# Fused attention, Fourier mixing, MLP and gated convolution: who multiplies and who adds the five taps of the gate's causal convolution

## The chip, the cores and the metric

The kernel runs on one core of a Trainium2 chip. The metric is the device time of one execution in microseconds (us), lower is better. TensorE (PE in the profile) does the matrix products, VectorE (DVE), ScalarE (ACT) and GpSimd (POOL) the element-wise work, and SyncE (SP) issues the DMA transfers.

## The reference

Three layers, one behind the other, on 4 batch entries of 576 positions and 512 features.

```python
x = out_up + out_local        # attention over pooled q, k, v, plus a band of 7 keys around each position
u = x + real(fft(fft(x, axis=1), axis=2))
un = (u - mu) / sqrt(var + 1e-06)
x = u + maximum(un @ w_ch1, 0) @ w_ch2              # 512 -> 2048 -> 512
xp = concatenate([zeros(B, 4, D), x], axis=1)
gate_pre = sum over k in 0..4 of conv_w[k] * xp[:, k:k + S, :]
gate = 1 / (1 + exp(-gate_pre))
out = (gate * (x @ w_val)) @ w_out
```

The convolution is depthwise and causal: tap k multiplies the signal shifted by 4 - k positions with one weight for each feature, so tap 4 is the position itself.

## The kernel before

**Layout.** Features lie on the 128 partitions, in 4 blocks of 128; X holds the 576 positions of a batch entry behind 4 columns of zeros. All the work behind the attention goes in 12 *units*, (b, j) for 4 batch entries and 3 pieces of UT = 192 positions. W is a list of 128x1024 weight tiles; the matrices are split into two fp16 halves each, and a product takes three passes of matmuls. W_n in the lists of instructions is such a tile; a weight piece that goes from the raw 64-bit form to float32 (`to_f32`) takes three VectorE instructions, one of line 283 (a shift and a mask) and two `stt` (line 165 is the `stt` helper, `scalar_tensor_tensor`; line 171 is the `add` helper, line 168 `mul`). `conv_w` then scales a piece and splits it.

**A unit's MLP** (`mlp_steps`). `h_group(g)`, g = 0 to 7, makes 24 matmuls of ph; ScalarE writes the upper half hh of its relu, VectorE the lower half hl with one `stt` that reads PSUM and hh. `c_group(g)`, 24 matmuls of pc with hh and hl, stands two h_groups behind, so TensorE runs c_group(0), h_group(2), c_group(1) and so on. Unit 0 is of another form (`steps32`, lines 1009 and 1022): float32 products without hh and hl. So the first hl is unit 1's.

**A unit's gated convolution** (`moe2_steps`). `conv(t)` is called for t = 4, 0, 1, 2, 3. Tap 4 starts the sum g; each call makes four products of 128x192, one for each block of features. In the units 1 to 10 the sum lies in the last weight tile, W_121 in the rows; in the first and the last unit it lies in a buffer of the pool `tap`. That pool has 3 buffers, which the products of the taps, the fp16 pair yy (`split_y`, line 1099 and an `stt`) and the output tile osb share. Then come `sigm`, `val(0)` and `val(1)` (24 matmuls each with yy; an `stt` that multiplies with the gate; the pair gh, gl), and `out_tile` (products with w_out, osb, and the store to out_dram). The last unit alone, by `LASTV`, already multiplies and adds on VectorE.

**What lies between.** The convolution of a unit lies in the MLP of the next one, unit 0's taps thus at the beginning of unit 1. The attention, Fourier and normalization steps of the batch entries 1 to 3 are put between the units. In the low-resolution attention, sc are scores in PSUM, nm their negated maximum, E the exponentials by ScalarE (line 682), then eT and po. `pooled_v` sums pieces of v in three additions on GpSimd (vr, ptv; line 171) and squares each loaded piece (v, v4 and a number) on ScalarE (line 425) behind that. In the Fourier part fs are sums and differences, fF folds (line 787), FH and FL their fp16 pair, which TensorE takes as ab. The normalization (`ln`) has uc, sq, sums st and two Newton steps r on VectorE; its column sums lie on GpSimd in most units. In the units 0 and 1 the rest of the weights comes in too: w_val and w_out by tiles raw, in two buffers, converted by VectorE.

**What sets the order.** Each step has a position in `put` and `spread`; the steps are called by position, and the scheduler of the framework then orders the instructions of each engine by a timeline of its own, with the operands' and buffers' dependencies as semaphores. Each engine runs its own list in order. All loads and stores are issued by SP, in order too: an issue that waits for a buffer holds up those behind it.

Of the kernel before, what the change touches and what calls it, by code (L numbers as in the profile page):

```python
# [9 lines left out]
F32 = mybir.dt.float32  # L10
# [3 lines left out]
AF = mybir.ActivationFunctionType  # L14
ALU = mybir.AluOpType
AX = mybir.AxisListType

B, H, S, D = 4, 8, 576, 64
# [3 lines left out]
UT = 192  # L22
UPB = S // UT
# [50 lines left out]
LASTV = True  # L74
# [53 lines left out]
def attn_moe_kernel(ctx, tc, q_t, k_t, v_t, w1, w2, w_val, conv_t, w_out, c_feat, c_seq, c_band, c_eye, out):  # L128
    nc = tc.nc
    P = 128  # L130
# [21 lines left out]
    V, A, G, T = nc.vector, nc.scalar, nc.gpsimd, nc.tensor  # L152
# [11 lines left out]
    def stt(eng, out, in0, scalar, in1, op0, op1):  # L164
        return eng.scalar_tensor_tensor(out=out, in0=in0, scalar=scalar, in1=in1, op0=op0, op1=op1)  # L165
# [4 lines left out]
    def add(eng, out, a, b):  # L170
        return eng.tensor_tensor(out=out, in0=a, in1=b, op=ALU.add)  # L171
# [24 lines left out]
    cw = const.tile([P, 4, 5], F32, name="cw")  # L196
# [717 lines left out]
    mainp = {}  # L914
# [173 lines left out]
    def moe2_steps(b, j):  # L1088
        i = b * UPB + j
        steps = []  # L1090
        m_ = {}
# [11 lines left out]
        def conv(t):  # L1103
            X = st[b]["X"]
            st[b]["taps"] = st[b].get("taps", 0) + 1
            c0 = PAD + j * UT - 4 + t
            if t == 4:
                if i in (0, B * UPB - 1):
                    g = mainp["tap"].tile([P, 4, UT], F32, tag="tap", name="tap")
                else:  # L1110
                    g = W[NPOS][:, 0:4 * UT].rearrange("p (a t) -> p a t", a=4)
            elif not (LASTV and i == B * UPB - 1):
                g = mainp["tap"].tile([P, 4, UT], F32, tag="tap", name="tap")
            last = LASTV and i == B * UPB - 1
            for c in range(4):
                if last and t == 4:
                    V.tensor_scalar(out=g[:, c], in0=X[:, c, c0:c0 + UT], scalar1=cw[:, c, t:t + 1], scalar2=None,
                                    op0=ALU.mult)
                elif last:
                    m = m_["g"][:, c]  # L1120
                    stt(V, m, X[:, c, c0:c0 + UT], cw[:, c, t:t + 1], m, ALU.mult, ALU.add)
                else:
                    A.activation(out=g[:, c], in_=X[:, c, c0:c0 + UT], func=AF.Copy, scale=cw[:, c, t:t + 1])  # L1123
            if last and t < 4:
                return
            if t == 4:
                m_["g"] = g
            else:
                add(G, m_["g"], m_["g"], g)

        def sigm():
            A.activation(out=m_["g"], in_=m_["g"], func=AF.Tanh, scale=0.5)
# [49 lines left out]
        def sof(b):  # L1182
# [4 lines left out]
            return d["sof"]  # L1187

        taps = [scale_out] + [lambda t=t: conv(t) for t in (4, 0, 1, 2, 3)] + [sigm]
        vals = [lambda: val(0), lambda: val(1)]  # L1190
        if i < B * UPB - 2:
# [59 lines left out]
    c0, c1 = st[0]["cuts"]  # L1251
# [101 lines left out]
```

## Time and profile before

| | before |
|---|---|
| median of 3 runs (lowest to highest) | 771.54 us (769.82 to 771.86) |
| the profiled execution, its own time | 768.35 us |
| its span | 766.5 us |
| mean granted TensorE clock | 0.93 |
| busy: PE / DVE / ACT / POOL | 91% / 59% / 49% / 24% |

The span goes from the first to the last instruction that the profiler saw in one execution; busy shares are shares of it. The granted clock is 1.00 at the upper level of TensorE's clock, 2.4 GHz, and 0.50 at the lower one, 1.2 GHz. Up to about 185 us the first attention, the loading of weights and unit 0 run. The first hl of the units 1 to 11 start at 197, 250, 306, 366, 429, 482, 538, 592, 632, 673 and 712 us.

### The profile page before, as it was taken

What the parts mean: (1) busy time and instruction counts of PE and PEld (TensorE: products, weight loads), DVE (VectorE), ACT (ScalarE), POOL (GpSimd) and SP (SyncE); (2) the same over time, 40 slices, a digit from 0 to 9 for tenths busy, and PEclk for the clock granted to TensorE, in tenths of its full rate; (3) what the DMA queues carried; (4) which work ended last, traced back from release to release, by engine and by line L of the source; (5) the groups of instructions that cost most, each with busy time, mean ns of one, the idle gap of its engine ahead of it and who ended that gap; (6) DMA issues with size and microseconds to landing.
All of it is one profiled execution on the core that took longest, in us unless ns stands there. A gap on an engine that the chain in (4) does not pass through costs nothing.

```text
span 766.5 us, 18498 instructions
## 1 busy us (share of the span) xinstructions
PE 695.8 (91%) x7811; PEld 605.4 (79%) x7811; DVE 450.3 (59%) x897; ACT 378.1 (49%) x1170; POOL 183.8 (24%) x187
## 2 busy tenths in 40 slices
PE   6869579986699998999979999898999999999996
PEld 3535459985688987987869899788799998999893
DVE  3894789769885766256786631656742472532134
ACT  1465211778544636677552766864522435251512
POOL 0400000015421522361231243601410323030300
PEclk8565579999799999999999999999899999999999
DMA  9965347033321110222121001001100000000001
GB/s 227 370 226 166 112 185 208 24 101 117 102 74 56 55 64 16 54 93 77 39 69 64 16 23 34 22 2 54 55 15 2 16 1 30 2 15 2 29 1 42
DMA packets 29004, 54.79 MB, mean 71 GB/s; under 512 B 2133, under 2 KB 17109, under 8 KB 27898
## 3 DMA queue, kind: packets, MB, share of 16 engines
q1 hardware_dynamic: 28922, 53.61, 21.6%
q8 instruction: 61, 1.00, 0.5%
q14 instruction: 21, 0.17, 0.1%
HBM read 46.52 MB, written 9.45 MB: 73 GB/s over the span
## 4 chain that ended last, share of the span: by engine, by line
PE 61%; DVE 20%; ACT 8%; DMA 7%; issue 1%; SPq 1%; POOL 0%; ACTq 0%; DVEq 0%; POOLq 0%
PE pc L1065 19%; PE ph L1047 18%; DVE W L165 6%; PE val L1144 5%; PE out L1160 5%; ACT dP L536 3%; PE po L716 2%; DMA v<-in_v_dram 2%; DVE W L283 2%; DVE fF L787 1%; ACT tap L1123 1%; PE dO L577 1%; PE sc L668 1%; DMA raw<-in_moe_w_out_dram 1%; PE ab L810 1%
## 5 line engine op out<-in xcount | busy, mean ns | idle before, releaser
L1065 PE MATMUL pc<-hh,W 128*128 128x192 f16 x1408 | 199.4, 248 | 3.8 <-ACT hh L1051 3.8
L1065 PEld LDWEIGHTS <-W 128*128 128x128 f16 x2112 | 178.0, 99 | 25.6 <-issue 21.8
L1047 PE MATMUL ph<-uh,W 128*128 128x192 f16 x1408 | 196.4, 247 | 0.1
L1065 PE MATMUL pc<-hl,W 128*128 128x192 f16 x704 | 173.3, 249 | 12.7 <-DVE hl L165 12.7
L1047 PEld LDWEIGHTS <-W 128*128 128x128 f16 x2112 | 176.4, 98 | 7.1 <-issue 5.1
L1047 PE MATMUL ph<-ul,W 128*128 128x192 f16 x704 | 173.7, 247 | 0.0
L171 POOL TENSOR_TENSOR W<-W,tap 128x768 f32<-128x768 f32 x40 | 74.9, 1873 | 141.2 <-ACT tap L1123 109.8
L165 DVE SCALAR_TENSOR_TENSOR hl<-ph,hh 128x384 f16<-128x384 f32 x88 | 48.0, 551 | 98.4 <-ACT hh L1051 98.2
L1051 ACT ACTIVATE hh<-ph 128x384 f16<-128x384 f32 x88 | 42.3, 485 | 72.0 <-PE ph L1047 71.6
L1123 ACT ACTIVATE tap<-X,cw 128x192 f32<-128x192 f32 x180 | 66.5, 446 | 5.5 <-DMA out_dram<-osb 4.7
L1144 PE MATMUL val<-yy,W 128*128 128x192 f16 x576 | 53.3, 246 | 4.0 <-ACT yy L1099 2.3
L1144 PEld LDWEIGHTS <-W 128*128 128x128 f16 x576 | 48.0, 98 | 5.1 <-issue 3.9
L536 ACT ACTIVATE dP<-dS,dmx 128x64 f32<-128x64 f32 x160 | 47.7, 332 | 0.3
L1160 PE MATMUL out<-W,gh 128*128 128x512 f16 x144 | 45.9, 379 | 0.0
L536 ACT ACTIVATION_READ_ACCUMULATOR dP<-dS,dmx 128x1 f32 x160 | 36.2, 226 | 0.0
L1160 PE MATMUL out<-W,gl 128*128 128x512 f16 x72 | 27.3, 379 | 2.1 <-DVE gl L165 2.1
L165 DVE SCALAR_TENSOR_TENSOR W<-W,W 128x1024 int32<-128x1024 int32 x24 | 28.7, 1215 | 0.1
L171 POOL TENSOR_TENSOR vr<-v 72x256 f32<-72x256 f32 x12 | 11.3, 944 | 66.9 <-DMA v<-in_v_dram 64.2
L165 DVE SCALAR_TENSOR_TENSOR yy<-X,s_y,yy 128x768 f16<-128x768 f32 x12 | 19.2, 1601 | 13.5 <-ACT yy L1099 13.4
L682 ACT ACTIVATE E<-sc,nm 72x144 f32<-72x144 f32 x64 | 23.5, 372 | 4.8 <-PE po L716 4.7
L716 PE MATMUL po<-ET,vr 72*64 72x144 f32 x128 | 21.6, 345 | 4.6 <-ACT ET L711 4.6
L1009 PE MATMUL ph<-u,W 128*128 128x192 f32 x128 | 24.8, 350 | 1.0 <-DVE u L945 1.0
(222 smaller groups left out, 1212.4 us busy)
## 6 DMA issues: line engine op xcount, KB each, us to landing
W<-in_moe_w_ch_dram SPq DMA_DIRECT2D x12, 1024.0 KB
v<-in_v_dram SPq DMA_DIRECT2D x32, 144.0 KB
out_dram<-osb SPq DMA_DIRECT2D x18, 256.0 KB
vw<-in_v_dram SPq DMA_DIRECT2D x16, 256.0 KB
X<-in_q_dram SPq DMA_DIRECT2D x6, 576.0 KB
kT<-in_k_dram SPq DMA_DIRECT2D x4, 582.0 KB
dx<-X SPq DMA_DIRECT2D x4, 576.0 KB
dr<-dx SPq DMA_DIRECT2D x4, 576.0 KB
```

The source lines that it names most:

```text
L165: return eng.scalar_tensor_tensor(out=out, in0=in0, scalar=scalar, in1=in1, op0=op0, op1=op1)
L171: return eng.tensor_tensor(out=out, in0=a, in1=b, op=ALU.add)
L536: A.activation(out=s_[:, z, a], in_=pss[par][:, z, a], func=AF.Exp, scale=SCALE, bias=mx[:, par, z, a:a + 1], accum_out=su[:, par, z, a:a ...
L682: A.activation(out=E[:, qc], in_=ps[:, qc], func=AF.Exp, scale=SCALE / 16, bias=nm[:, qc:qc + 1], accum_out=su[:, qc:qc + 1],)
L716: T.matmul(out=po[par * 64:par * 64 + 64], lhsT=d["vr"][:, kc, (a % 2) * 4 + (a // 2) * 2 + par], rhs=ets[par][:, kc], start=(kc == 0), st ...
L1009: i = T.matmul(out=ps[:, e], lhsT=W[kc * 2 + m // 8 + 1][:, o:o + 128], rhs=u()[:, kc, :], start=(kc == 0), stop=(kc == 3))
L1047: T.matmul(out=ps[:, e], lhsT=w1_ap(pw, kc, 2 * g + e), rhs=uh[px][:, kc, :], start=(t == 0), stop=(t == 11))
L1051: A.activation(out=h_, in_=ps, func=AF.Relu)
L1065: T.matmul(out=ps[m // 2][:, m % 2], lhsT=w2_ap(pw, kk, m), rhs=x[px][:, e, :], start=(kk == 0 and (pw, px) == (0, 0) and m % 2 == 0), sto ...
L1123: A.activation(out=g[:, c], in_=X[:, c, c0:c0 + UT], func=AF.Copy, scale=cw[:, c, t:t + 1])
L1144: T.matmul(out=ps[:, e], lhsT=wv_ap(pw, kc, 2 * mh + e), rhs=m_["y"][px][:, kc, :], start=(t == 0), stop=(t == 11))
L1160: T.matmul(out=ps, lhsT=(gh, gl)[px][:, kc, t * 128:(t + 1) * 128], rhs=wo_ap(pw, kc), start=(n == 0), stop=(n == 11))
```

## The change

The taps 0 to 3 are no longer multiplied by ScalarE into a buffer of their own and added by GpSimd: VectorE does both with one `stt` for each block of features, in place, out = x * w + out. Tap 4 stays ScalarE's product (VectorE's in the last unit, as before). The buffers for the four other products fall away.

```diff
--- before.py
+++ after.py
@@ -1109,24 +1109,16 @@
                     g = mainp["tap"].tile([P, 4, UT], F32, tag="tap", name="tap")
                 else:
                     g = W[NPOS][:, 0:4 * UT].rearrange("p (a t) -> p a t", a=4)
-            elif not (LASTV and i == B * UPB - 1):
-                g = mainp["tap"].tile([P, 4, UT], F32, tag="tap", name="tap")
+                m_["g"] = g
             last = LASTV and i == B * UPB - 1
             for c in range(4):
-                if last and t == 4:
-                    V.tensor_scalar(out=g[:, c], in0=X[:, c, c0:c0 + UT], scalar1=cw[:, c, t:t + 1], scalar2=None,
-                                    op0=ALU.mult)
+                x, w, m = X[:, c, c0:c0 + UT], cw[:, c, t:t + 1], m_["g"][:, c]
+                if t < 4:
+                    stt(V, m, x, w, m, ALU.mult, ALU.add)
                 elif last:
-                    m = m_["g"][:, c]
-                    stt(V, m, X[:, c, c0:c0 + UT], cw[:, c, t:t + 1], m, ALU.mult, ALU.add)
+                    V.tensor_scalar(out=m, in0=x, scalar1=w, scalar2=None, op0=ALU.mult)
                 else:
-                    A.activation(out=g[:, c], in_=X[:, c, c0:c0 + UT], func=AF.Copy, scale=cw[:, c, t:t + 1])
-            if last and t < 4:
-                return
-            if t == 4:
-                m_["g"] = g
-            else:
-                add(G, m_["g"], m_["g"], g)
+                    A.activation(out=m, in_=x, func=AF.Copy, scale=w)
 
         def sigm():
             A.activation(out=m_["g"], in_=m_["g"], func=AF.Tanh, scale=0.5)
```

The scheduler orders the lists anew. Three places are shown; lines behind the edit have numbers lower by 8 in the changed kernel.

VectorE around the first hl, that of unit 1, before (tap is the gate's sum or a product, W_117 and W_118 are pieces of w_ch2, W_120 and W_121 pieces of w_val and w_out on their way from raw):

```order
L165 SCALAR_TENSOR_TENSOR W_117<-W_118,s_w_1528,W_117 128x1024
L165 SCALAR_TENSOR_TENSOR W_120<-raw,W_120 128x512 x2
L283 TENSOR_SCALAR W_120<-raw 128x512
L165 SCALAR_TENSOR_TENSOR W_120<-raw,W_120 128x512 x2
L945 TENSOR_TENSOR uc<-X,st 128x768
L283 TENSOR_SCALAR W_121<-raw 128x512
L165 SCALAR_TENSOR_TENSOR W_118<-W_118,s_w_1528 128x1024
L165 SCALAR_TENSOR_TENSOR hl<-ph,hh 128x384
```

and of the change:

```order
L165 SCALAR_TENSOR_TENSOR W_117<-W_118,s_w_1528,W_117 128x1024
L165 SCALAR_TENSOR_TENSOR tap<-X,cw,tap 128x192 x3
L165 SCALAR_TENSOR_TENSOR W_120<-raw,W_120 128x512
L165 SCALAR_TENSOR_TENSOR tap<-X,cw,tap 128x192 x4
L165 SCALAR_TENSOR_TENSOR W_120<-raw,W_120 128x512
L165 SCALAR_TENSOR_TENSOR tap<-X,cw,tap 128x192 x2
L945 TENSOR_TENSOR uc<-X,st 128x768
L165 SCALAR_TENSOR_TENSOR W_118<-W_118,s_w_1528 128x1024
L165 SCALAR_TENSOR_TENSOR tap<-X,cw,tap 128x192
L283 TENSOR_SCALAR W_120<-raw 128x512
L165 SCALAR_TENSOR_TENSOR hl<-ph,hh 128x384
```

Ten multiply-adds now stand ahead of this hl; the shift of W_121 moved behind it, and the second shift of W_120 stands right in front of it.

TensorE at the same place, as a difference (pc_2100 is the accumulator whose second matmul reads hl):

```order
 L1047 LDWEIGHTS W_114
 L1047 MATMUL ph<-uh,W_114 128x192
-L939 MATMUL st<-uc,ones 128x192
 L1065 LDWEIGHTS W_115
 L1065 MATMUL pc_2100<-hh,W_115 128x192
 L1065 LDWEIGHTS W_115
 L1065 MATMUL pc_2101<-hh,W_115 128x192
+L668 MATMUL sc<-qkT 72x144 x4
 L1065 LDWEIGHTS W_115
 L1065 MATMUL pc_2100<-hl,W_115 128x192
```

A sum of squares' or means' st moved forward, and four score products sc stand ahead of the first matmul that reads hl. ScalarE at the same place, as a difference (v_1851 is a loaded piece of v, ssv its sum of squares):

```order
 L1051 ACTIVATE hh<-ph 128x384
-L1123 ACTIVATE tap<-X,cw 128x192 x4
-L1051 ACTIVATE hh<-ph 128x384
-L1123 ACTIVATE tap<-X,cw 128x192 x4
-L951 ACTIVATE sq<-uc 128x768
-L682 ACTIVATE E,lsu<-sc,nm 72x144
 L425 ACTIVATE v_1851,ssv<-v_1851 72x512
-L682 ACTIVATE E,lsu<-sc,nm 72x144
+L682 ACTIVATE E,lsu<-sc,nm 72x144 x4
 L425 ACTIVATE v_1862,ssv<-v_1862 72x512
```

Eight products of taps are gone from here, and the four exponentials E stand in one piece behind the square of v_1851.

SP's list of loads at the same time, before (v4 are pieces of v, raw those of the raw weights):

```order
L186 DMA v4_1808<-in_v_dram 72x2x256
L188 DMA v4_1850<-in_v_dram 72x2x256
L188 DMA raw_2095<-in_moe2_w_val_dram 128x1024
L188 DMA raw_2259<-in_moe2_w_out_dram 128x1024
L188 DMA v4_1851<-in_v_dram 72x2x256
L188 DMA v4_1862<-in_v_dram 72x2x256
L188 DMA raw_2230<-in_moe2_w_val_dram 128x1024
```

and of the change:

```order
L186 DMA v4_1808<-in_v_dram 72x2x256
L188 DMA v4_1850<-in_v_dram 72x2x256
L188 DMA v4_1851<-in_v_dram 72x2x256
L188 DMA raw_2095<-in_moe2_w_val_dram 128x1024
L188 DMA v4_1862<-in_v_dram 72x2x256
L188 DMA v4_1863<-in_v_dram 72x2x256
L188 DMA raw_2259<-in_moe2_w_out_dram 128x1024
L188 DMA raw_2230<-in_moe2_w_val_dram 128x1024
```

v4_1851 moved in front of raw_2095, and v4_1862 and v4_1863 in front of raw_2259.

VectorE in one of the late units, from the end of the unit ahead (X takes the sums pc), before:

```order
L165 SCALAR_TENSOR_TENSOR X<-pc_8650,iv_1544,X 128x2x192
L165 SCALAR_TENSOR_TENSOR X<-pc_8651,iv_1544,X 128x2x192
L165 SCALAR_TENSOR_TENSOR hl<-ph,hh 128x384 x3
L165 SCALAR_TENSOR_TENSOR yy<-X,s_y_9134,yy 128x768
L165 SCALAR_TENSOR_TENSOR hl<-ph,hh 128x384 x2
L165 SCALAR_TENSOR_TENSOR W_121<-W_121,val 128x384
```

and of the change:

```order
L165 SCALAR_TENSOR_TENSOR X<-pc_8584,iv_1544,X 128x2x192
L165 SCALAR_TENSOR_TENSOR X<-pc_8585,iv_1544,X 128x2x192
L165 SCALAR_TENSOR_TENSOR W_121<-X,cw,W_121 128x192 x7
L165 SCALAR_TENSOR_TENSOR hl<-ph,hh 128x384
L165 SCALAR_TENSOR_TENSOR W_121<-X,cw,W_121 128x192 x4
L165 SCALAR_TENSOR_TENSOR hl<-ph,hh 128x384
L165 SCALAR_TENSOR_TENSOR W_121<-X,cw,W_121 128x192 x5
L165 SCALAR_TENSOR_TENSOR yy<-X,s_y_9062,yy 128x768
L165 SCALAR_TENSOR_TENSOR hl<-ph,hh 128x384 x3
```

The sixteen multiply-adds stand among the first hl of the unit, in pieces of seven, four and five.

## Rows read from the trace of the kernel before

**Rows 1.** The page, busy time and share of each engine.

```profile
PE 695.8 (91%) x7811; PEld 605.4 (79%) x7811; DVE 450.3 (59%) x897; ACT 378.1 (49%) x1170; POOL 183.8 (24%) x187
```

**Rows 2.** Windows of 40 us; the first row names the columns.

```profile
core 0: us, PE busy (x) PEld busy (x) DVE busy (x) ACT busy (x) POOL busy (x), PEclk, DMA share, GB/s
160.00:200.00 40.00, 25.20 (x284) 23.05 (x283) 32.77 (x37) 33.27 (x97) 17.28 (x13) 0.81 0.27 90
...
360.00:400.00 40.00, 34.70 (x385) 30.47 (x384) 31.02 (x49) 22.16 (x60) 12.77 (x8) 1.00 0.18 52
...
520.00:560.00 40.00, 36.15 (x376) 31.76 (x374) 26.87 (x43) 19.61 (x45) 13.23 (x12) 0.91 0.18 59
...
600.00:640.00 40.00, 40.00 (x444) 37.27 (x443) 24.19 (x41) 17.15 (x37) 12.39 (x11) 1.00 0.02 9
```

**Rows 3.** Timeline, TensorE: start, length, instruction [idle before, its releaser].

```profile
197.55 0.32 PE L1065 MATMUL pc<-hl,W 128*128 128x192 f16 x1 [9.33 <-DVE hl L165]
```

**Rows 4.** Timeline, VectorE, 177 to 198 us.

```profile
177.18 1.28 DVE L165 SCALAR_TENSOR_TENSOR W<-W,s_w 128x1024 f16<-128x1024 f32 x1
...
180.97 0.41 DVE L283 TENSOR_SCALAR W<-raw 128x512 int32<-128x512 int32 x1
...
182.50 1.82 DVE L165 SCALAR_TENSOR_TENSOR W<-raw,W 128x512 int32<-128x512 int32 x2
184.77 2.86 DVE L283 TENSOR_SCALAR W<-raw 128x512 int32<-128x512 int32 x1 [0.45 <-DMA raw<-in_moe_w_val_dram]
...
190.90 0.94 DVE L945 TENSOR_TENSOR uc<-X,st 128x768 f32<-128x768 f32 x1
191.76 2.53 DVE L283 TENSOR_SCALAR W<-raw 128x512 int32<-128x512 int32 x1
194.21 2.82 DVE L165 SCALAR_TENSOR_TENSOR W<-W,s_w 128x1024 f16<-128x1024 f32 x1
196.95 0.55 DVE L165 SCALAR_TENSOR_TENSOR hl<-ph,hh 128x384 f16<-128x384 f32 x1
```

**Rows 5.** Timeline, GpSimd, 181 to 196 us.

```profile
181.78 1.99 POOL L171 TENSOR_TENSOR vr<-v 72x256 f32<-72x256 f32 x1 [8.22 <-DMA v<-in_v_dram]
...
185.55 3.75 POOL L171 TENSOR_TENSOR tap<-tap 128x768 f32<-128x768 f32 x2
...
192.20 3.75 POOL L171 TENSOR_TENSOR tap<-tap 128x768 f32<-128x768 f32 x2
```

**Rows 6.** Groups by line: instruction and count | busy, mean ns | idle before.

```profile
L1123 ACT ACTIVATE tap<-X,cw 128x192 f32<-128x192 f32 x180 | 66.5, 446 | 5.5 <-DMA out_dram<-osb 4.7 <-POOL W L171 0.5 <-DVE X L165 0.2
...
L1123 ACT ACTIVATE W<-X,cw 128x192 f32<-128x192 f32 x40 | 15.8, 449 | 19.0 <-DVE X L165 17.8 <-DVE gl L165 0.9 <-DVE W L165 0.4
...
L171 POOL TENSOR_TENSOR W<-W,tap 128x768 f32<-128x768 f32 x40 | 74.9, 1873 | 141.2 <-ACT tap L1123 109.8 <-ACT W L1123 30.3
...
L165 DVE SCALAR_TENSOR_TENSOR tap<-X,cw,tap 128x192 f32<-128x192 f32 x16 | 5.7, 405 | 0.0
```

**Rows 7.** Chain of waits, 180 us: start, length, what.

```profile
180.05 4.70 DMA raw<-in_moe_w_val_dram
```

**Rows 8.** Timeline, SP's issues of v.

```profile
178.26 0.33 SPq L186 DMA_DIRECT2D v<-in_v_dram  x1
...
184.89 1.89 SPq L188 DMA_DIRECT2D v<-in_v_dram  x2
```

**Rows 9.** Timeline, ScalarE, an exponential.

```profile
192.62 0.36 ACT L682 ACTIVATE E<-sc,nm 72x144 f32<-72x144 f32 x1
```

**Rows 10.** Window behind the wait for hl, columns as in rows 2.

```profile
197.50:202.20 4.70, 4.65 (x30) 4.39 (x30) 4.18 (x10) 2.69 (x7) 0.32 (x1) 0.50 0.32 106
```

**Rows 11.** Timeline, VectorE, two Newton steps.

```profile
388.32 0.35 DVE L165 SCALAR_TENSOR_TENSOR r<-r,r 128x192 f32<-128x192 f32 x1
...
389.10 1.87 DVE L165 SCALAR_TENSOR_TENSOR r<-r,vv 128x192 f32<-128x192 f32 x1
```

**Rows 12.** Timeline, ScalarE, products of a tap at 395 us.

```profile
395.21 1.49 ACT L1123 ACTIVATE tap<-X,cw 128x192 f32<-128x192 f32 x4 [3.92 <-DMA out_dram<-osb]
```

**Rows 13.** Chain of waits, late unit, one group of matmuls.

```profile
678.94 1.98 PE pc L1065 x24
```

## The prediction, made before the changed kernel ran

> **What bounds the kernel now.** I read the page's busy shares first, then stretches of 40 us, then what TensorE waited for, then VectorE, GpSimd and ScalarE around each such wait. TensorE is busy 91% of the span and VectorE, the next, 59% [rows 1]. Those are averages over stages. In the late units TensorE has no gap at all: 40.00 us of 40 between 600 and 640, while VectorE is busy 24.2, ScalarE 17.2 and GpSimd 12.4 [rows 2]. There a change on the other engines can only cost, never gain. Between 160 and 200 TensorE works 25.20 us of 40, between 360 and 400 it works 34.70, between 520 and 560 it works 36.15 [rows 2]. That is 14.8, 5.3 and 3.85 us of idle time, and whatever this change brings has to come out of such stretches. In the third, VectorE is held up by GpSimd's differences and squares, which stay; I count nothing for it, nor for the smaller gaps between.
>
> The large gap is one wait: at 197.55 a matmul of pc starts that had waited 9.33 us for hl from VectorE [rows 3], that is since 188.22. VectorE was never idle before that hl. It was slow. A shift (line 283) that takes 0.41 us at 180.97 takes 2.86 at 184.77 and 2.53 at 191.76; a weight conversion that takes 1.28 at 177.18 takes 2.82 at 194.21 [rows 4]. GpSimd is at work in all these moments: a sum of v, then two tap additions from 185.55 to 189.3, two more from 192.20 to 195.95 [rows 5]. So the four tap additions of unit 0 hold VectorE up, and TensorE with it. The Trainium skill ("SBUF — State Buffer", Who interferes with whom) gives this a rule: a VectorE instruction in a two-port mode or with two SBUF inputs and a GpSimd instruction that reads SBUF exclude each other for a whole instruction. The 2.86 against 0.41 agrees with it.
>
> **The change, part by part.** *ScalarE* loses 16 of 20 products in each of 11 units. 220 took 66.5 + 15.8 = 82.3 us, so 0.374 each [rows 6], and 176 of them are 65.8 us. ScalarE was not what TensorE waited for in the large gap, so I count nothing for this by itself.
>
> *GpSimd* loses all 44 additions: 74.9 us for forty [rows 6] and two pieces of 3.75 for the other four [rows 5], 82.4 us in all. GpSimd's own time is on no path that I found; what counts is that VectorE is no longer held by them.
>
> *VectorE* gains 176 multiply-adds. The last unit already does this work there: 16 of them in 5.7 us, 0.356 each [rows 6]. That is 62.7 us, 5.7 per unit. In the full stretches it lies beside TensorE's work (VectorE 24.2 + 5.7 of 40 [rows 2]); without that cover it would be 5.7 us a unit.
>
> *Unit 0's taps, the gap at 188.* They lie in unit 1's beginning. The order after shows ten of the sixteen multiply-adds ahead of the first hl, and one shift and one weight piece now behind it. Three things can be last.
> First, VectorE's queue. From 182.50 it has two weight pieces (1.82, the measured time, in part already held), ten multiply-adds (3.56), uc (0.94), a conversion (1.28) and a shift (0.41): 8.0 us, so hl starts at 190.5 instead of 196.95 [rows 4]. TensorE started 0.60 us after hl did, so it resumes at 191.1.
> Second, on SP the load of raw_2095, which that shift reads, now stands behind v4_1851. It was issued at 180.05 and took 4.70 [rows 7]. v4_1851 could not be issued before 184.89, when its buffer came free [rows 8]; so raw_2095 lands at 189.6 or a little later, and hl starts at 190.0. This is just covered.
> Third, TensorE now has the next four score matmuls (sc) ahead of the first matmul with hl, and their PSUM buffers are freed by ScalarE's exponentials, which stand behind the square of v4_1851. A v load issued at 178.26 was used at 181.78, 3.5 us later [rows 5, 8]; so v4_1851 is there at 188.4, its sum on GpSimd takes up to 1.99 [rows 5], four exponentials at 0.36 [rows 9] make 191.8, and 193.9 if the load and the sum are as slow again as they were quick here.
> TensorE thus resumes between 191.1 and 193.9. I take 192.75, near the later end, since the third chain has the most links: a gain of 4.8 us (3.6 to 6.4).
>
> *The clock behind that gap.* From 197.5 to 202.2 TensorE's granted clock is 0.50, the lower of its two levels (1.2 of 2.4 GHz) [rows 10]: 4.7 us of work that would have been 2.35 at the upper one. It fell during the idle 9.33 us. The idle time will be about half as long; whether the clock then falls no row tells. Bounds 0 and 2.35, taken 1.2.
>
> *Units 3 and 4, 360 to 400.* Here a Newton step of the normalization that takes 0.35 at 388.32 takes 1.87 at 389.10, and the one after it the like [rows 11], under two tap additions on GpSimd; they stand in front of the FL that TensorE waits for. And ScalarE stands 3.92 us until an output store frees a tap buffer, then makes four products (1.49) before yy, which TensorE waits for next [rows 12]. Both causes are gone: the additions, and the buffers that each tap took from the pool that output and yy also use. The first is worth two times 1.5 us. Bounds: 0, if GpSimd's half of the transform is as late, and 5.3, the whole idle time of the stretch [rows 2]. Taken 3.0.
>
> *What the multiply-adds cost elsewhere.* In the late units seven stand in a row ahead of an hl: 2.5 us. A block of hl is wanted two groups of 24 matmuls after its turn, and a group takes 1.98 [rows 13], so there are about 4.0 us. Seven alone are covered. They read two SBUF tiles, and where GpSimd works at the same moment they can be held as the Newton step was, 1.5 us each time: 2.5 + 1.5 = 4.0 is just covered, two such holds lose 1.5. I take one such loss, 1.5 us in all, in the range from 0 to one per unit.
>
> **Sum.** The profiled execution took 768.35 us, 1.85 around its span of 766.5. 768.35 - 4.8 - 1.2 - 3.0 + 1.5 = 760.85. The runs shown have their median at 771.54, 3.19 above it, so I forecast 764.0. Taking all lower bounds (6.4 + 2.35 + 5.3, no loss) gives 757.5 on that scale.
>
> **Rivals.**
> *The wait only moves (no change).* Line 283's shift of the next raw weights stands in VectorE's queue ahead of later hl, and on SP raw_2259 goes from two places ahead of v4_1862 to behind v4_1863. If that load lands late, TensorE, ahead by 5 us at 193, waits for a later hl instead and has lost the lead by about 225. Then 4.8 + 1.2 go and 1.5 net of the rest stays: 770.0. For it: each raw load takes 4.70 us and there are only two buffers [rows 7]. Against it: the order also moves other work of VectorE in front, and TensorE has no wait that long anywhere behind 200 in which the loads show. The Trainium skill's "Perfetto Trace Analysis" (Optimizing Scalar/DVE Operations) warns in the same direction: the two engines share an SBUF port, so handing work from one to the other might not help. By that sentence, too, about nothing would change.
>
> *VectorE is held in every unit (slower).* One mechanism: the multiply-adds ahead of hl, held by what GpSimd still does (sums of v, squares, the transform's differences, normalizations). If each of the ten units behind the first has two holds, it loses 1.5 us, 15 us in all against 9.0 gained: 774.35, or 777.5 on the scale of the median. It decides from 0.9 us per unit on. By the rule of the page "SBUF — State Buffer" in the Trainium skill every multiply-add is exposed to such a hold, since it has two SBUF inputs. For it: the 1.87 against 0.35 [rows 11] is such an instruction. Against it: GpSimd is left with little in the late units, where TensorE is full and VectorE idle for 40% [rows 2].
>
> *More than forecast.* All gaps close and the clock stays up: 757 or below.
>
> **Chances.** A median within 0.3%, 2.3 us, can't be told from no change. Forecast (757.5 to 769.2): 0.66. More than that: 0.04. The wait only moves, or gains and holds cancel (769.2 to 773.9): 0.15. Held in every unit, or a like loss (above 773.9): 0.15. Faster 0.70, same 0.15, slower 0.15. The likeliest case has its range from 757 to 769; the range that leaves out no more than 2 in 10 goes from 757 to 774.
>
> **What would show it.** In the profile after: multiply-adds at about 0.36 each on VectorE and no tap additions on GpSimd; the line 283 shift back at 0.4 us around 185 to 192 except beside sums of v; the wait for hl of 9.33 us down to 3 to 6; less than 2.5 us of lower clock behind it; between 360 and 400 TensorE busy for 37 us or more; 600 to 640 still full. I would be wrong if a new wait of several us for hl or a raw load shows between 195 and 230, if the sc matmuls hold TensorE past 194, or if short waits for hl show in each late unit with multiply-adds of more than 1 us in front of them.

## The result, and the profile after

The changed kernel took 750.85 us (median of 4, 750.29 to 754.8) against 770.68 for the kernel before: a ratio of 0.9757, 95% interval 0.9716 to 0.9797. Run once more beside the later experiments it took 752.54 (ratio 0.9786, 0.9771 to 0.9801). The gain is thus 16.5 to 20 us. The prediction was 764.0, with a range of 757 to 774: right in sign, wrong in size by 13 us and outside its range.

The page of the changed kernel, busy times, answers to [rows 1]. ScalarE has lost 57 us and GpSimd 76, VectorE gained 32:

```profile
PE 688.4 (92%) x7811; PEld 599.7 (80%) x7811; DVE 482.2 (64%) x1073; ACT 321.0 (43%) x994; POOL 108.2 (14%) x143
```

The multiply-adds alone were to add 63 us to VectorE. Its count grew by just these 176 (897 to 1073), its busy time by half of that, so its other instructions took less time than before. Windows of 40 us of the changed kernel (columns as in [rows 2]; the stretches hold somewhat earlier work than those of before, since the kernel runs ahead):

```profile
160.00:200.00 40.00, 31.16 (x357) 28.23 (x356) 33.33 (x60) 29.57 (x83) 15.06 (x13) 0.91 0.23 75
360.00:400.00 40.00, 39.77 (x448) 35.48 (x446) 31.74 (x59) 15.29 (x31) 7.66 (x12) 1.00 0.25 82
440.00:480.00 40.00, 34.94 (x452) 31.42 (x450) 20.25 (x44) 21.06 (x66) 13.53 (x17) 0.91 0.07 22
520.00:560.00 40.00, 39.80 (x435) 35.02 (x433) 27.57 (x60) 13.41 (x28) 6.29 (x13) 1.00 0.11 35
600.00:640.00 40.00, 40.00 (x444) 37.04 (x443) 21.65 (x46) 12.53 (x22) 4.26 (x6) 1.00 0.04 15
```

TensorE's idle time between 360 and 400 is gone (5.30 to 0.23), that between 520 and 560 as well (3.85 to 0.20), and the late unit is as full as it was. One stretch, 440 to 480, has become worse (0.83 us of idle time before, 5.06 now). What TensorE waited for from 175 to 748 us, summed by releaser, before (us in total, times, longest):

```profile
PE pc L1065 <- DVE hl L165: 12.7, 4, 9.3
PE pc L1065 <- ACT hh L1051: 3.8, 2, 2.0
PE ab L810 <- DVE FL L165: 3.6, 2, 2.6
PE st L939 <- ACT X L583: 2.4, 3, 1.6
PE val L1144 <- ACT yy L1099: 2.3, 2, 1.3
```

and in the changed kernel:

```profile
PE pc L1065 <- DVE hl L165: 5.1, 2, 3.5
PE st L939 <- ACT X L583: 4.6, 3, 4.0
...
PE ph L1047 <- ACT uh L973: 1.6, 1, 1.6
...
PE pc L1065 <- ACT hh L1051: 1.2, 1, 1.2
...
PE ab L810 <- DVE FL L165: 0.2, 1, 0.2
```

The waits for hl fell by 7.6 us, those for FL by 3.4, those for yy are gone, those for hh fell by 2.6. A wait for ScalarE's X grew. VectorE ahead of the first hl, in the changed kernel (start, length; answers to [rows 4]):

```profile
179.06 0.41 DVE L283 TENSOR_SCALAR W<-raw 128x512 int32<-128x512 int32 x1
...
180.58 1.54 DVE L165 SCALAR_TENSOR_TENSOR tap<-X,cw,tap 128x192 f32<-128x192 f32 x3
182.05 1.21 DVE L165 SCALAR_TENSOR_TENSOR W<-raw,W 128x512 int32<-128x512 int32 x1
183.18 1.86 DVE L165 SCALAR_TENSOR_TENSOR tap<-X,cw,tap 128x192 f32<-128x192 f32 x4
...
189.56 0.95 DVE L283 TENSOR_SCALAR W<-raw 128x512 int32<-128x512 int32 x1
190.43 0.55 DVE L165 SCALAR_TENSOR_TENSOR hl<-ph,hh 128x384 f16<-128x384 f32 x1
```

The shifts of line 283 take 0.41 and 0.95 us; those of 2.5 to 2.9 are gone. TensorE waits twice here, first for X, then briefly for hl:

```profile
183.24 0.69 PE L939 MATMUL st<-uc,ones 128*128 128x192 f32 x1 [4.00 <-ACT X L583]
...
191.03 0.24 PE L1065 MATMUL pc<-hl,W 128*128 128x192 f16 x1 [1.60 <-DVE hl L165]
```

### The profile page after: what moved, and what is told of

It is laid out like the page before. It is cut to its first block, busy times and chain, and to the rows that moved or that the text cites. A ratio compares the mean times of both kernels' runs of the same rounds, so it can differ in the third digit from the quotient of the medians.

```text
span 749.1 us, 18445 instructions
## 1 busy us (share of the span) xinstructions
PE 688.4 (92%) x7811; PEld 599.7 (80%) x7811; DVE 482.2 (64%) x1073; ACT 321.0 (43%) x994; POOL 108.2 (14%) x143
## 4 chain that ended last, share of the span: by engine, by line
PE 59%; DVE 22%; DMA 9%; ACT 6%; POOL 2%; issue 1%; SPq 1%; DVEq 0%; POOLq 0%; ACTq 0%
PE pc L1065 20%; PE ph L1047 19%; DVE W L165 8%; PE out L1152 5%; PE val L1136 5%; ACT dP L536 3%; DMA v<-in_v_dram 2%; PE po L716 2%; DVE tap L165 2%; PE ab L810 1%; DMA dr<-dx 1%; DMA dx<-X 1%; DMA X<-in_moe_w_ch_dram 1%; DMA raw<-in_moe_w_ch_dram 1%; DVE fF L787 1%
## 5 line engine op out<-in xcount | busy, mean ns | idle before, releaser
L1065 PE MATMUL pc<-hh,W 128*128 128x192 f16 x1408 | 196.1, 247 | 1.2 <-ACT hh L1051 1.2
L1065 PEld LDWEIGHTS <-W 128*128 128x128 f16 x2112 | 176.7, 98 | 14.4 <-issue 10.8
L165 DVE SCALAR_TENSOR_TENSOR W<-X,cw,W 128x192 f32<-128x192 f32 x160 | 61.0, 437 | 2.3 <-ACT W L1121 2.2
L1152 PEld LDWEIGHTS <-gh 128*128 128x128 f16 x144 | 14.2, 99 | 14.4 <-issue 0.9
L1009 PE MATMUL ph<-u,W 128*128 128x192 f32 x128 | 24.3, 345 | 1.0 <-DVE u L945 1.0
L668 PE MATMUL sc<-qkT 64*72 64x144 f32 x128 | 22.4, 341 | 2.5 <-DVE qkT L588 1.0
L1143 ACT ACTIVATE gh<-W 128x384 f16<-128x384 f32 x20 | 10.6, 528 | 31.9 <-DVE W L165 31.8
L1121 ACT ACTIVATE W<-X,cw 128x192 f32<-128x192 f32 x40 | 15.5, 455 | 19.6 <-DVE X L165 17.8
```

The costliest lines, as they stand in the source:

```text
L668: T.matmul(out=pss[par][:, qc], lhsT=d["qkT"][r, 0, a, qc * QC:(qc + 1) * QC], rhs=d["qkT"][r, 1, a, :], start=True, stop=True,)
L1009: i = T.matmul(out=ps[:, e], lhsT=W[kc * 2 + m // 8 + 1][:, o:o + 128], rhs=u()[:, kc, :], start=(kc == 0), stop=(kc == 3))
L1065: T.matmul(out=ps[m // 2][:, m % 2], lhsT=w2_ap(pw, kk, m), rhs=x[px][:, e, :], start=(kk == 0 and (pw, px) == (0, 0) and m % 2 == 0), sto ...
L1121: A.activation(out=m, in_=x, func=AF.Copy, scale=w)
L1152: T.matmul(out=ps, lhsT=(gh, gl)[px][:, kc, t * 128:(t + 1) * 128], rhs=wo_ap(pw, kc), start=(n == 0), stop=(n == 11))
```

## The experiments

A ratio below is always to the kernel before, on the same chip and in the same hour. Of each edit only the lines that matter are shown; the pool of the buffer `dum` is left out.

**Which engine's relief is it?** First the two halves of the change, each alone. *add_on_dve*: ScalarE keeps its products and the tap buffers, VectorE makes the additions.

```diff
-                add(G, m_["g"], m_["g"], g)
+                add(V, m_["g"], m_["g"], g)
```

> As before, ScalarE makes all five products into tap buffers, but the 44 additions are done by VectorE in place of GpSimd. Theory A (GpSimd's additions hold VectorE, and TensorE behind it): the holds are gone, VectorE pays 44 additions of about 0.9 us; 752 to 759 us. Theory B (what helps is that ScalarE is relieved of 176 products and the tap buffers are freed): nothing of that is done here; 768 to 773 us. Theory C (the new order of the lists, whatever the engines): no number of its own, any time between.

Measured 765.65 us, ratio 0.9954 (0.9930 to 0.9978). Between the theories: with the additions off GpSimd the gain is about 4 us of the 16.5 to 20. That is a net figure. VectorE has the 44 additions now, and it stands idle in front of them for ScalarE's products, a wait that was GpSimd's before [rows 6]:

```profile
L171 DVE TENSOR_TENSOR W<-W,tap 128x768 f32<-128x768 f32 x40 | 39.0, 974 | 32.2 <-ACT tap L1123 31.8
```

*mul_on_dve*: VectorE makes the products into the tap buffers, GpSimd adds.

```diff
+                elif t < 4:
+                    V.tensor_scalar(out=g[:, c], in0=X[:, c, c0:c0 + UT], scalar1=cw[:, c, t:t + 1], scalar2=None,
+                                    op0=ALU.mult)
```

> VectorE makes the products of the taps 0 to 3 into tap buffers in place of ScalarE, GpSimd adds them as before. Theory A: the additions still hold VectorE, which has more work (176 products of 0.31 us) to be held; 768 to 778 us. Theory B: ScalarE is relieved as in the change; 752 to 760 us, a little more than the change since the buffers are still used.

Measured 777.0 us, ratio 1.0096 (1.0062 to 1.0130): slower. With GpSimd's additions still there, relieving ScalarE in this way brings nothing. The products are held too (438 ns in the mean, 311 in the median, 1919 the longest), and VectorE now waits for a tap buffer in ScalarE's place, 6.3 us in all. That group (busy, mean ns, idle time before it):

```profile
L1123 DVE TENSOR_SCALAR tap<-X,cw 128x192 f32<-128x192 f32 x176 | 66.6, 438 | 6.9 <-DMA out_dram<-osb 6.3 <-POOL AL L828 0.3 <-POOL W L171 0.2
```

*dummy_adds*: the changed kernel, with GpSimd's 44 additions put back as additions of X that nothing reads.

```diff
+            if t < 4 and not last:
+                z = mainp["dum"].tile([P, 4, UT], F32, tag="dum", name="dum")
+                y = X[:, :, c0:c0 + UT]
+                add(G, z, y, y)
```

> The changed kernel, and beside each tap of its multiply-adds GpSimd makes one addition of 128x768 of X with itself into a buffer that nothing reads, 44 in all, as many as were removed. Theory A: VectorE is held again, and the multiply-adds too; 765 to 778 us. Theory B: GpSimd was on no path, so the time of the change; 749 to 754 us.

Measured 800.4 us, ratio 1.0401 (1.0368 to 1.0434): 50 us above the changed kernel, far more than theory A said. Nothing reads the result, so what the work costs is what it holds up. TensorE waits for GpSimd itself only 1.4 us in that trace; it waits for VectorE. The group of multiply-adds and the wait for hl there:

```profile
L165 DVE SCALAR_TENSOR_TENSOR W<-X,cw,W 128x192 f32<-128x192 f32 x160 | 89.1, 611 | 2.2 <-ACT W L1125 2.0
```

```profile
PE pc L1065 <- DVE hl L165: 32.1, 10, 10.0
```

611 ns for one against 437 in the changed kernel, and TensorE waits 32.1 us for hl, also in the late units that never waited before. This is the second rival of the prediction (VectorE held in every unit), made to happen.

*no_taps*: no product and no addition for the taps 0 to 3 in the units 0 to 10, so the gate's sum is tap 4 alone there.

```diff
-                if t < 4:
+                if t < 4 and not last:
+                    pass
+                elif t < 4:
                     stt(V, m, x, w, m, ALU.mult, ALU.add)
```

> The taps 0 to 3 are left out in all units but the last (no product, no addition), so neither ScalarE nor GpSimd nor VectorE has that work. What it is below the changed kernel is the price of the 176 multiply-adds on VectorE. Theory A with the multiply-adds all covered by TensorE: 746 to 751 us. If each unit pays for them: 15 us less than the change or more, below 737 us.

Measured 749.93 us, ratio 0.9757 (0.9720 to 0.9793), the ratio of the changed kernel itself. The 176 multiply-adds, some 69 us of VectorE in the changed kernel, cost nothing that can be measured. That holds for the total: its lists are ordered anew, and its trace has a wait of 3.2 us for the exponentials that the changed kernel has not, while the wait of 3.50 for hl shown below is gone from it.

**What of ScalarE, what of the buffers?** The additions on VectorE gave 4 us, the change 16.5 to 20. For the rest ScalarE's time and the three buffers that taps, yy and osb share come into question. *stt_bufs*: the changed kernel, with the multiply-adds of the taps 0 to 2 writing into tap buffers in turn.

```diff
+            if t < 4 and not last:
+                src = m_["z"] if t else m_["g"]
+                dst = m_["g"] if t == 3 else mainp["tap"].tile([P, 4, UT], F32, tag="tap", name="tap")
+                for c in range(4):
+                    stt(V, dst[:, c], X[:, c, c0:c0 + UT], cw[:, c, t:t + 1], src[:, c], ALU.mult, ALU.add)
+                m_["z"] = dst
+                return
```

> The changed kernel, but the multiply-adds of the taps 0 to 2 write into buffers of the pool tap in turn instead of in place (the fourth writes back to the sum), so the pool is loaded by the taps much as before, while ScalarE and GpSimd stay relieved. The run with additions on VectorE showed that taking the holds away alone gives about 4 us of 19; this one asks whether the buffers give the rest. Theory B2 (the buffers that taps, yy and osb share are what the relief needs): 758 to 767 us. Theory B1 (ScalarE's time, not the buffers): 750 to 754 us.

Measured 761.12 us, ratio 0.9896 (0.9878 to 0.9913): 9 to 10 us of the gain are gone though every engine does what it does in the change. ScalarE's timeline in that kernel shows one place of it:

```profile
391.07 0.94 ACT L1099 ACTIVATE yy<-X,s_y 128x768 f16<-128x768 f32 x1 [7.09 <-DMA out_dram<-osb]
```

ScalarE stands 7.09 us in front of yy, with hh and everything else queued behind it, until an output store has landed and frees a buffer. TensorE waits 6.3 us of them for yy. Over the whole execution ScalarE stands 19.2 us in front of yy for stores, against 4.7 us in front of the products in the kernel before [rows 6]. So this run loads the pool more heavily than the kernel before did: it shows that the buffers can cost, not what they cost there.

*dummy_act*: the changed kernel, with ScalarE's 176 products made again into a buffer of their own that nothing reads.

```diff
+            if t < 4 and not last:
+                z = mainp["dum"].tile([P, 4, UT], F32, tag="dum", name="dum")
+                for c in range(4):
+                    A.activation(out=z[:, c], in_=X[:, c, c0:c0 + UT], func=AF.Copy, scale=cw[:, c, t:t + 1])
```

> The changed kernel, and with each tap ScalarE makes the four products again, into a buffer of their own that nothing reads, 176 in all. GpSimd stays relieved and the pool tap is not loaded. Theory B1 (ScalarE's queue delays what TensorE waits for): 758 to 768 us. Theory B2 (only the buffers): 750 to 754 us.

Measured 763.46 us, ratio 0.9917 (0.9890 to 0.9944), about 11 to 13 us of the gain gone. ScalarE's timeline there, at the beginning of unit 1:

```profile
187.00 0.63 ACT L425 ACTIVATE v<-v 72x512 f32<-72x512 f32 x1 [5.49 <-POOL vr L171]
...
190.23 1.48 ACT L1117 ACTIVATE dum<-X,cw 128x192 f32<-128x192 f32 x4
191.61 0.47 ACT L1051 ACTIVATE hh<-ph 128x384 f16<-128x384 f32 x1
```

and TensorE's:

```profile
188.30 1.01 PE L939 MATMUL st<-uc,ones 128*128 128x192 f32 x2 [7.10 <-ACT X L583]
192.14 0.48 PE L1065 MATMUL pc<-hh,W 128*128 128x192 f16 x2 [2.51 <-ACT hh L1051]
```

The wait of 2.51 for hh is ScalarE's: four products of 1.48 stand right in front of it. The 7.10 are not. There ScalarE itself waited for a sum of v on GpSimd (below), and 7.10 against 4.00 is some 3 us of the 11 to 13 that must not be put down to ScalarE's time.

In the changed kernel, then, both can cost time. What they cost in the kernel before has to be asked from its side. *tap4* is the kernel before with a fourth tap buffer; *add_dve_tap4* has that and the additions on VectorE.

```diff
-        for n, bufs in (("un", 2), ("hg", 3), ("g", 1), ("L", 2), ("tap", 3), ("S", 3)):
+        for n, bufs in (("un", 2), ("hg", 3), ("g", 1), ("L", 2), ("tap", 4), ("S", 3)):
```

> The kernel before with four buffers in the pool tap in place of three; the engines' work is the same. If the shared buffers cost time by themselves, also under GpSimd's holds: 760 to 767 us. If they only cost once the holds are gone: 768 to 772.

Measured 768.45 us, ratio 0.9993 (0.9970 to 1.0015): nothing.

> The additions on VectorE with ScalarE's products, now with four buffers in the pool tap. Against the 765.65 us with three: the buffers' part comes back, 757 to 762 us, if yy and osb waiting for a buffer is what kept that run slow; 764 to 767 if it is ScalarE's time alone.

Measured 758.78 us, ratio 0.9873 (0.9857 to 0.9890), against 0.9954 with three buffers. The same buffer that was worth nothing under GpSimd's additions is worth 6 us without them. The group of yy, with three buffers (add_on_dve):

```profile
L1099 ACT ACTIVATE yy<-X,s_y 128x768 f16<-128x768 f32 x12 | 11.2, 937 | 9.4 <-DVE X L165 4.9 <-DMA out_dram<-osb 4.5
```

and with four (add_dve_tap4), where the wait for the store falls from 4.5 to 1.4:

```profile
L1099 ACT ACTIVATE yy<-X,s_y 128x768 f16<-128x768 f32 x12 | 11.2, 933 | 6.3 <-DVE X L165 4.9 <-DMA out_dram<-osb 1.4
```

The traces show where. The table has TensorE's idle time (us) in five profiled executions. A stretch goes from the last pc matmul of one unit's MLP to that of the next; the last two rows count from the last matmul of unit 0's MLP to the end:

| | before | tap4 | add_on_dve | add_dve_tap4 | changed |
|---|---|---|---|---|---|
| unit 0 to unit 1 | 13.6 | 12.8 | 10.1 | 7.6 | 7.0 |
| unit 3 to unit 4 | 5.3 | 5.8 | 6.0 | 1.6 | 0.2 |
| unit 5 to unit 6 | 2.6 | 2.7 | 2.5 | 2.7 | 5.1 |
| unit 6 to unit 7 | 3.9 | 0.9 | 1.0 | 0.0 | 0.2 |
| idle from unit 0's last matmul on | 36.6 | 32.5 | 31.1 | 24.3 | 24.3 |
| time from unit 0's last matmul on | 588.9 | 586.6 | 588.2 | 576.8 | 575.0 |

From unit 3 to unit 4 neither half helps alone. With only the buffer, TensorE waits 3.1 us for FL, which VectorE delivers late. With only the additions gone, it waits for yy, in front of which ScalarE has stood 4.51 us until a store landed:

```profile
394.87 0.24 PE L1144 MATMUL val<-yy,W 128*128 128x192 f16 x1 [4.21 <-ACT yy L1099]
```

With both, no wait there is longer than 0.8 us. With four buffers the lists ahead of unit 0's taps differ too: the last matmul of unit 0 starts at 179.0 and 179.3, against 177.6 before. In these executions, then, the result of tap4 is 2.3 us gained behind that matmul and 1.7 lost ahead of it.

**Which units?** *only_unit0* has the change in unit 0 alone, *not_unit0* in the units 1 to 10 alone (the others as before); the second has `i == 0` where the first has `i > 0`.

```diff
+            if t < 4 and not last and (i > 0):
+                z = mainp["tap"].tile([P, 4, UT], F32, tag="tap", name="tap")
+                for c in range(4):
+                    A.activation(out=z[:, c], in_=X[:, c, c0:c0 + UT], func=AF.Copy, scale=cw[:, c, t:t + 1])
+                add(G, m_["g"], m_["g"], z)
+                return
```

> Only unit 0's taps are multiplied and added by VectorE; the units 1 to 10 are as before. It measures the first term of the prediction alone: by the prediction 4.8 us and 1.2 us of clock, so 764 against 770; by the trace of the changed kernel 6.6 us less idle time at that place, 763. If later waits take it back (the rival in which the wait only moves): 768 to 771.

Measured 764.22 us, ratio 0.9935 (0.9915 to 0.9956): 5.6 us, by the difference of the medians.

> The change in the units 1 to 10; unit 0's taps as before, so the wait of 9 us for the first hl stays. If the places add up, 19 us less the 6 of unit 0: 756 to 759 us. By the prediction (3.0 less 1.5 for the rest): 768.

Measured 761.01 us, ratio 0.9895 (0.9876 to 0.9914): 8.8 us, where the prediction had 1.5. The parts give 14.4 of 16.5 to 20 us. The profile of only_unit0 has a candidate for 3 us of what is missing: up to the first hl its lists are those of the change, but its sum of v on GpSimd took 4.51 us where the change's took 0.95,

```profile
181.36 4.51 POOL L171 TENSOR_TENSOR vr<-v 72x256 f32<-72x256 f32 x1 [9.24 <-DMA v<-in_v_dram]
185.96 0.72 POOL L171 TENSOR_TENSOR vr<-vr,ptv 72x256 f32<-72x256 f32 x1
```

and TensorE's wait for X behind it was 7.50, not 4.00:

```profile
187.21 0.69 PE L939 MATMUL st<-uc,ones 128*128 128x192 f32 x1 [7.50 <-ACT X L583]
```

Whether the changed kernel has executions like this was the question of *after_again*, the changed kernel unaltered.

> The changed kernel once more, unaltered, with more rounds. Its first wait behind ScalarE's X was 4.0 us, that of the kernel with only unit 0 changed 7.5 us with the same lists up to there. If the two are states that either kernel can be in, some runs here lie about 3.5 us above the others, as one of four did: a spread of 750 to 755 us. If it was the kernel: all within 750 to 752.

Measured 752.54 us, 751.79 to 753.89 in four runs; its profiled execution waited 4.08 us there. Runs that lie 3.5 us apart did not show here, though one of the first four (754.8) lay 3.9 above the next. So that explanation stays a guess, and where the 2 to 5.5 us between the parts and the whole come from stays open.

**Is it the order alone?** All lists are ordered anew by any edit. *before_shift* and *after_shift* put every unit's taps 0.05 of a unit later.

```diff
-P_TAP = (-0.05, 0.35)
+P_TAP = (0.0, 0.4)
```

> The kernel before with every unit's five taps put 0.05 of a unit (about 2.4 us) later in the program order (P_TAP 0.0 to 0.4); same work on the same engines. Theory C (it is the order of the lists that decides, any reshuffle moves the time by several us): below 763 or above 777. If the loads of the engines and the buffers decide: 766 to 774.

> The changed kernel with the same shift of the taps. Theory C (the changed kernel happened on a good order): 756 to 768. If loads and buffers decide: 749 to 755.

Measured 770.65 us (ratio 1.0000, 0.9983 to 1.0018) and 754.12 us (0.9784, 0.9759 to 0.9808). The kernel before does not move, and the changed one keeps the ratio of its second measurement. One such shift of each kernel thus shows nothing of theory C.

**Can it be had better?** *v_on_dve*: the sums of v go to VectorE as well; *v_ln_dve*: the column sums of the normalization too (`eng = V`).

```diff
-                add(G, t, x4[0], x4[1])
-                add(G, o, x4[2], x4[3])
-                add(G, o, o, t)
+                add(V, t, x4[0], x4[1])
+                add(V, o, x4[2], x4[3])
+                add(V, o, o, t)
```

> The changed kernel with the sums of v (36 additions of 72x256) on VectorE in place of GpSimd as well. In the profile of the changed kernel these sums are beside the multiply-adds at the two waits that are left for hl (1.6 us at 191, 3.5 us at 471 with some 2.5 us of lower clock behind it), and at 183 ScalarE's X waits behind one. If GpSimd and VectorE holding each other is what is left: 741 to 748 us. If VectorE's queue, 13 us longer, comes to bound there: 751 to 758.

> As the run before, and the column sums of the normalization on VectorE in all units too, so that GpSimd keeps the differences of the transform and little else. Holds gone on both sides: 739 to 748 us. VectorE's queue bounds: 751 to 760.

Measured 749.54 us (748.13 to 749.95; ratio 0.9725, 0.9708 to 0.9743) and 752.27 us (0.9753, 0.9728 to 0.9778). All four runs of the first lie below the eight of the changed kernel, 2.3 us below their median of 751.85. That is less than expected. The eight were measured at other times, though, and the interval of the ratio overlaps that of the change's first measurement (0.9716 to 0.9797), so a gain is not shown. The second brings nothing more. TensorE's waits from 175 to 748 us in v_on_dve:

```profile
PE st L939 <- ACT X L583: 3.9, 3, 2.0
PE sc L668 <- ACT E L682: 3.2, 1, 3.2
PE pc L1065 <- DVE hl L165: 3.1, 4, 1.5
```

The waits for X and hl shrink; a wait of 3.2 for ScalarE's exponentials takes their place, the chain that the prediction had put last at unit 1.

## Why the prediction was wrong

*Unit 0's taps.* Right in sum: 4.8 and 1.2 of clock were forecast, 5.6 measured alone. Inside it three things differed, so the good sum is partly luck. VectorE's queue ended the wait for hl, as the first of the three chains had it (190.5 forecast, 190.43 measured, with its list some 2 us earlier than before: 179.06 against 180.97 for the first shift shown); the chain over v, the exponentials and sc, for whose sake 192.75 was taken, showed as 0.15 us. The wait of 9.33 did not shrink to one of 3 to 6 us: 1.60 stayed at hl, and a wait of 4.00 for X stands ahead of it, where the kernel before had 1.57. In ScalarE's list X stands behind the square of a piece of v, which waits for that piece's load and its sum on GpSimd. And the clock gave nothing back: from 183.2 to 188.2 it was granted at 0.50 with 4.81 us of work, as long as in [rows 10].

*The multiply-adds elsewhere.* Forecast 1.5 us of loss; no_taps shows none in the total. They took 0.38 us each (160 in 61.0 us) where 0.36 was forecast. They are held, as expected, where GpSimd still sums v: eight of them take 5.39 us in front of an hl, and TensorE stands 3.50.

```profile
464.82 5.39 DVE L165 SCALAR_TENSOR_TENSOR W<-X,cw,W 128x192 f32<-128x192 f32 x8
470.13 0.55 DVE L165 SCALAR_TENSOR_TENSOR hl<-ph,hh 128x384 f16<-128x384 f32 x1
```

But it is offset by a like wait of before that is gone, 2.90 us for hl at 538, with the clock at 0.57 for the 8 us around either.

*Units 3 and 4.* Forecast 3.0 of a possible 5.3 us; the stretch from 360 to 400 gave 5.07, close to the bound. Both causes named, the held Newton steps [rows 11] and the wait for the store [rows 12], were real. But the 3.0 was the price of the Newton steps alone, and taking only the additions away left TensorE's idle time there at 6.0 us.

*The step that failed* is the count for the units 1 to 10: 3.0 less 1.5, where not_unit0 measured 8.8. Two of its terms were too small. The wait for a tap buffer was named at one place and given no price, as if it went along with the holds. The runs show that it is the second half of the same relief: a buffer alone 0.9993, the additions off GpSimd alone 0.9954, both 0.9873. And for the third stretch the prediction counted "nothing for it, nor for the smaller gaps between", since GpSimd's differences and squares stay there. They stayed, and yet its idle time (unit 6 to unit 7) fell from 3.9 us to 0.2 in the change and to 1.0 or less with either half alone.

*ScalarE.* "I count nothing for this by itself" was judged at one wait and then applied to all units; whether it failed stays open. Against it speaks dummy_act, with 11 to 13 us of which some 3 are not ScalarE's, and the wait for hh, which fell from 3.8 to 1.2. For it speaks that add_dve_tap4, in which ScalarE still makes every product, has the idle time of the change from unit 0's last matmul on and is only 1.8 us longer there. The rest of the distance between their two spans (755.8 and 749.1) lies ahead of that matmul, which starts at 179.0 in the one and at 174.1 in the other. So the step from 0.9873 to 0.9757 or 0.9786 can't be put down to ScalarE.

*Part of the 13 us is no step of it.* The medians differ by more than the profiled executions, 19.8 against 17.4 us of span. And of those 17.4, about 3.5 were there before the MLP of unit 1: the last matmul of unit 0 started at 177.6 in the profiled execution of before and at 174.1 in that of the change, partly because the clock fell to 0.57 from 168 to 172 in the first and stayed at 1.00 in the second. In the experiments that moment lay between 174.1 and 179.3. What is left, 13.9 us, is what stands against the 7.5 of the forecast. Whether the 3.5 belong to the change or to these two executions no run shows.

*The rivals.* That the wait only moves was true in part, at X (4.00 at 183) and at an hl (3.50 at 470), and took back only a part of the gain. That VectorE is held in every unit needed GpSimd's additions to be there: dummy_adds is that case, at 1.04. The work handed over cost nothing on VectorE (no_taps), and GpSimd's cost 50 us beside it (dummy_adds). The sentence of the Trainium skill ("Perfetto Trace Analysis", Optimizing Scalar/DVE Operations), that offloading between GpSimd and VectorE might not help, did not come true in this direction.

## What to carry to other kernels

Where two engines hold each other up, price an operation on GpSimd by what VectorE does in that time, not by GpSimd's own busy share: additions that nothing waited for cost 50 us when they were put back. When one cause of a wait is taken away, ask what is late next at the same place, and price both together: a buffer that gave nothing under the holds gave 6 us without them. A stretch that holds idle time gets a range from nothing to all of it, also where the cause that was read there stays.

## What the runs showed of the hardware

The hold goes both ways, and for longer than one instruction. In only_unit0 the sum of v on GpSimd, 0.72 us for each of the two behind it, took 4.51 from 181.36 on. VectorE ran eleven instructions with two SBUF inputs back to back in that time, none of them slowed:

```profile
181.05 1.06 DVE L165 SCALAR_TENSOR_TENSOR tap<-X,cw,tap 128x192 f32<-128x192 f32 x3
182.04 0.68 DVE L165 SCALAR_TENSOR_TENSOR W<-raw,W 128x512 int32<-128x512 int32 x1
182.64 1.40 DVE L165 SCALAR_TENSOR_TENSOR tap<-X,cw,tap 128x192 f32<-128x192 f32 x4
183.96 0.68 DVE L165 SCALAR_TENSOR_TENSOR W<-raw,W 128x512 int32<-128x512 int32 x1
184.56 0.73 DVE L165 SCALAR_TENSOR_TENSOR tap<-X,cw,tap 128x192 f32<-128x192 f32 x2
```

In the changed kernel, with the same lists, GpSimd got through in 0.95 us and VectorE's pieces were slowed instead (1.54 for the first three). The Trainium skill ("SBUF — State Buffer", Who interferes with whom) says that the order of issue, not the form of the operation, decides who is blocked. The runs agree that either can lose, and show besides that the loser can be held over a whole row of the other's instructions. What made the difference between these two executions no run here shows.
